# Query norms spread by one product with ones instead of a diagonal, a product and a copy; the order of the plan set anew

## The chip, the cores and the metric

One core of one Trainium2 chip. The metric is the device time of one execution in microseconds (us); the profile covers one such execution and gives its span, from the first to the last instruction. Engines: TensorE (PE; PEld is its weight load), VectorE (DVE), ScalarE (ACT), GpSimd (POOL) and SyncE (SP), which here issues most of the DMAs.

## The reference, cut to what matters

Channel attention followed by a feed-forward net. Per batch (4 of them, 6080 tokens, 256 channels) the columns of q and k are divided by their norms over the tokens, `s = kn^T qn / tau` (256x256) goes through a softmax over its rows, and the attention matrix is multiplied with v:

```
qn = q / (norm(q, axis=1) + 1e-6);  kn = k / (norm(k, axis=1) + 1e-6)
a  = softmax(kn.T @ qn / tau)            # 256 x 256 per batch
x  = (v @ a).reshape(24320, 256)
out = (relu(x @ w_in) ** 2) @ w_out      # w_in 256x2048, w_out 2048x256
```

The change touches the part that turns the raw scores `k^T q` into `s`: every score is multiplied by one over the norm of its key channel (its row, a number per partition) and by one over the norm of its query channel (its column, the same row of 256 numbers on every partition).

## The kernel before, in words

All 24320 tokens are worked in 24 chunks (six per batch) and 8 pairs of hidden blocks per chunk, so 192 pairs, "quads" in the code. The attention matrix is folded into w_in once per batch, so a quad is products of v with folded weights (L714), relu, square, and products with w_out (L861). Products of two 2x2 block matrices use seven products in place of eight, and each fp32 number is split in a high and a low fp32r half (`split`, L340: a cast on ACT or DVE, then a subtraction on DVE), three products per pair of operands.

A planner in the kernel (class `Plan`, L55 to L240) writes the order out by hand. Each step (`add`) has a key, which is a place on a time axis where 1.0 is one quad, a set of engines that may run it with a cost in us for each, and what it reads and writes. PE, SP and POOL take the ready step with the lowest key that lies no further than `PLACE["ahead"]` beyond the next PE step; DVE and ACT take the one that is due first, worked back from PE's order. The result is a fixed list; on the chip every engine runs its list in order and waits where an input is late. So a step that takes longer than its cost in the plan holds everything behind it on its engine. The table `PLACE` (L22) holds the keys and offsets.

For batch 0 the start of the kernel loads k and q (L345), multiplies them in plain fp32 (L469, each product recorded as two instructions), and adds their squares on DVE (L447); meanwhile PE also takes early score products of batch 1 (tile o). For batches 1 to 3 the scores are collected while the quads of the batch before run (b=1 during batch 0 and so on), and the steps `norms`, `spread`, `exps`, `attnT` and `fold` for the next batch lie between the quads.

`norms` (L496): DVE adds the two halves of the squares (L500), PE sums them over the partitions by four products with one column of ones (L505), which gives [128, 4], the squared norms of two key and two query halves, one channel per partition. ACT takes the root (L512) and, on a dummy, an exp to load the next table (L515). DVE does seven small operations on 4 columns (L520 to L526, two of them reciprocals: a Newton step for the root, then the inverse), then makes two diagonal matrices (L529) of the query factors. `spread` (L533): PE multiplies ones with the diagonals (L537), so that every partition holds all 256 query factors, and ACT or DVE copies them (L317) to the tile zq. `exps` (L543): DVE multiplies the scores by both factors (L550) and takes the row maximum (L552), ACT does the exp (L555). `attnT` (L565) transposes on PE (L572), `fold` (L596, L607) multiplies with w_in.

The PSUM tile h has two buffers, shared by the quads' products and by the tiles of these steps; a buffer is free for the next product only when its last reader is done. Names such as h or g in the profile are tiles; several steps of helpers share one line (L342 is the subtraction of every split, L317 every copy and cast).

Of the kernel before, what the change touches and what calls it, by code (L numbers as in the profile page):

```python
# [15 lines left out]
AF = mybir.ActivationFunctionType  # L16
# [3 lines left out]
P = 128  # L20

PLACE = {'ahead': {'P': 2.08, 'A': 1.179, 'V': 1.2, 'S': 2.311, 'G': 2.0},  # L22
 'shy': {'V': 0.964},
 'look': 5,
 'push': 6.141,
 'bias': {'V': 0.0, 'A': 0.956},
 'later': (0.86, 0.5),
 'scores': (2.0, 1.23, 0.632, 0.301, 0.646, 2.436),
 'folds': (3.331, 4.0, 0.599, 0.454, 1.234, 1.7),
 'tokens': (-3.119, -2.668, -2.352, -0.817, -0.655, -0.6, -0.55),  # L30
 'weights': (1.573, -0.172),
 'behind': (3, 3),
 'sums': (0.872, 1.889, 2.975, 3.873, 4.9, 5.812, 6.84),
 'lead': 13,
 'start': (-0.157, -0.107, 0.46, 0.864, 1.067, 1.201, -0.301, -0.25, -0.1, 0.02, 0.472),
 'groups': ((0, 1, 2), (3, 4, 5, 6)),
# [206 lines left out]
def vec(n):  # L243
    return 0.07 + 0.00104 * n
# [6 lines left out]
def act(n):  # L251
    return 0.1 + 0.00083 * n
# [3 lines left out]
def tile_channel_attention_relu2_ffn(ctx, tc, kq, vT, tau, w_in, w_out, outT):  # L256
# [236 lines left out]
    def tiny(key, eng, cost, fn, r, w):  # L493
        add(key, {eng: cost}, lambda e: fn(), r, w)

    def norms(key, b):  # L496
        acc, bank = ("acc", b), plan.tile("h", ("nb", b))
        ny, nz, nd = (plan.tile("y", (k, b, k)) for k in ("y1", "y2", "zv"))
        diag = plan.tile("zq", ("diag", b))
        alu(key, 512, lambda: nc.vector.tensor_add(out=made[acc][:, 0], in0=made[acc][:, 0], in1=made[acc][:, 1]),  # L500
            [(acc, 0)], [(acc, 0)])

        def sums():
            for i in range(2 * NH):
# [5 lines left out]
        def roots():  # L510
            y = get(ny, [P, 2 * NH])
            nc.scalar.activation(out=y, in_=made[bank][:, :2 * NH], func=AF.Sqrt)  # L512

        tiny(key, "A", 1.7 if b else 0.3, roots, [(bank, 0)], [(ny, 0)])
# [16 lines left out]
        tiny(key, "V", 1.9, scales, [(bank, 0), (ny, 0), ("rtau", 0)], [(nz, 0), (nd, 0), (diag, 0)])  # L531

    def spread(key, b):  # L533

        diag, bank = ("diag", b), plan.tile("h", ("zb", b))
        zq = plan.tile("zq", ("zqs", b))
        tiny(key, "P", 0.45, lambda: nc.tensor.matmul(  # L537
            out=get(bank, [P, HMAX])[:, :C], lhsT=ones, rhs=made[diag].rearrange("p d c -> p (d c)"),
            start=True, stop=True), [(diag, 0)], [(bank, 0)])
        add(key, {"A": act(256), "V": vec(256)}, lambda e: copy(e, get(zq, [P, NH, P]).rearrange("p d c -> p (d c)"),  # L540
                                                               made[bank][:, :C]), [(bank, 0)], [(zq, 0)])

    def exps(key, b, s, stok):  # L543
        zq, zv, den = ("zqs", b), ("zv", b, "zv"), plan.tile("den", ("den", b))
        for h in range(NH):
            en, nm = plan.tile("e", ("e", b, h)), plan.tile("nm", ("nm", b, h))

            def scaled(h=h, en=en, nm=nm):
                e = get(en, [P, C])
                nc.vector.scalar_tensor_tensor(out=e, in0=s()[:, h * C:(h + 1) * C], scalar=made[zv][:, h:h + 1],  # L550
                                               op0=ALU.mult, in1=made[zq].rearrange("p d c -> p (d c)"), op1=ALU.mult)
                nc.vector.tensor_reduce(out=get(nm, [P, 1]), in_=e, op=ALU.max, axis=AX.X, negate=True)  # L552

            tiny(key, "V", 0.95, scaled, [(zq, 0), (zv, 0), *stok], [(en, 0), (nm, 0)])
            tiny(key, "A", 0.6, lambda h=h, en=en, nm=nm: nc.scalar.activation(  # L555
# [115 lines left out]
    def v_split(keys, ci):  # L671
# [10 lines left out]
        b11, b12, b21, b22 = ((v, h, t) for h in range(2) for t in range(2))  # L682
        sub, plus = nc.vector.tensor_sub, nc.vector.tensor_add
        alu(keys[0], T, lambda: sub(out=one(), in0=blk(0, 1), in1=blk(0, 0)), [b11, b12], [(t1, 0)])
        for key, i, fn, hv, tok, x, y, r in zip(
# [123 lines left out]
    def weight_sums(key, i):  # L809
# [181 lines left out]
    for i, (b, g) in enumerate(loads):  # L991
        at(-6.9 + 0.25 * g if b == 0 else -0.9 + 0.05 * g, first_load, i, b, g)
    s0, s1 = plan.tile("x", ("s0",)), plan.tile("o11", ("s1",))
# [49 lines left out]
    for b in range(1, B):  # L1043
# [102 lines left out]
```

## Time and profile before

| | |
|---|---|
| times of three runs | 2065.6, 2067.95, 2067.96 us; median 2067.95 |
| the profiled execution | 2064.93 us, its span 2063.0 us |
| PE busy | 2048.0 us, 99% of the span |
| DVE busy | 1990.6 us, 96% |
| ACT busy | 1715.3 us, 83% |
| DMA | 562.51 MB, mean 273 GB/s |
| granted TensorE clock | 1.0 |

Busy time is the union of an engine's instructions. In a timeline a row merges neighbouring instructions of one line: start, duration of the row, and in brackets the idle time of the engine before it and what ended it. Matmuls overlap one another in such a row, so the pitch of PE's work is read from one row's start to the next.

### The profile page before, as it was taken

Reading aid. Unit: us, or ns where it says so; the run is one execution under the profiler, and the core shown is the slowest. Engines: PE = TensorE matmul, PEld = TensorE weight load, DVE = VectorE, ACT = ScalarE, POOL = GpSimd, SP = SyncE. Lnnn points to the kernel's source line nnn. Section 1 sums busy time; section 2 is a strip of 40 time slices with the busy share of each in tenths; the row PEclk is TensorE's granted clock in tenths of the full one; section 3 lists DMA queues with packets and bytes.
Section 4 is the critical chain, followed back from the end, with each engine's and each line's share of the span. In section 5 each row is a group of like instructions: output and inputs, shape, how many; then the busy total and the mean of one; then the engine's idle time right before and its main releaser. Section 6 shows DMA issues by size and latency. Waiting matters only on the chain.

```text
span 2063.0 us, 29286 instructions
## 1 busy us (share of the span) xinstructions
PE 2048.0 (99%) x9419; PEld 1714.0 (83%) x9419; DVE 1990.6 (96%) x3199; ACT 1715.3 (83%) x2718; POOL 188.2 (9%) x220
## 2 busy tenths in 40 slices
PE   9999999999999999999999999999999999999998
PEld 7778888888888888888888888888888888888887
DVE  7999999999999999999999999999999999999998
ACT  6779898988898889898888888989888787787785
POOL 0000001100111111100011111110000000000010
PEclk9999999999999999999999999999999999999999
DMA  9979989878999999978899999997898887887885
GB/s 362 346 231 351 292 258 304 231 230 278 296 320 309 286 300 282 283 232 252 275 297 319 302 288 293 290 285 229 254 274 271 278 244 224 244 247 224 241 230 156
DMA packets 342249, 562.51 MB, mean 273 GB/s; under 512 B 27088, under 2 KB 240336, under 8 KB 342096
## 3 DMA queue, kind: packets, MB, share of 16 engines
q1 hardware_dynamic: 311424, 491.09, 70.2%
q0 software_dynamic: 30672, 69.55, 19.2%
q8 instruction: 76, 1.25, 0.2%
q14 instruction: 77, 0.63, 0.1%
HBM read 424.02 MB, written 66.98 MB: 238 GB/s over the span
## 4 chain that ended last, share of the span: by engine, by line
PE 97%; DVE 1%; ACT 1%; issue 0%; DMA 0%; SPq 0%; DVEq 0%; ACTq 0%
PE h L714 25%; PE o L861 24%; PE h L861 20%; PE z L714 12%; PE x L714 6%; PE x L469 6%; PE h L607 2%; PE o L469 1%; DMA kq<-kq 0%; ACT s L321 0%; DVE uM L908 0%; DVE hl L342 0%; DVE uM L969 0%; DVE D L752 0%; PE h L505 0%
## 5 line engine op out<-in xcount | busy, mean ns | idle before, releaser
L714 PE MATMUL h<-vt,wt 128*128 128x512 f32 (+1 forms) x2304 | 617.5, 389 | 3.7 <-ACT x L317 2.7
L714 PEld LDWEIGHTS h<-vt,wt 128*128 128x128 f32 x2304 | 429.6, 188 | 92.0 <-ACT x L317 4.2
L861 PE MATMUL o<-g,wo 128*128 128x512 f32 (+1 forms) x1746 | 466.4, 388 | 0.1
L861 PE MATMUL h<-hl,wo 128*128 128x512 f32 (+1 forms) x1608 | 392.8, 388 | 0.0
L861 PEld LDWEIGHTS o<-g,wo 128*128 128x128 f32 x1746 | 327.2, 188 | 66.4 <-DVE g L342 1.3
L861 PEld LDWEIGHTS h<-hl,wo 128*128 128x128 f32 x1608 | 301.2, 188 | 60.6 <-ACT m L317 0.4
L342 DVE TENSOR_TENSOR hl<-D,hl 128x512 fp32r<-128x512 f32 (+1 forms) x536 | 350.0, 675 | 0.4
L714 PE MATMUL z<-vt,wt 128*128 128x512 f32 (+1 forms) x1152 | 324.4, 390 | 1.1 <-ACT z L317 0.8
L342 DVE TENSOR_TENSOR g<-s,g 128x1024 fp32r<-128x1024 f32 (+1 forms) x225 | 271.0, 1204 | 3.8 <-ACT g L317 3.8
L476 POOL DMA_DIRECT2D D<-D x159 | 140.7, 903 | 1414.6 <-DVE hl L342 795.9
L714 PEld LDWEIGHTS z<-vt,wt 128*128 128x128 f32 x1152 | 213.7, 188 | 46.6 <-DVE D L752 2.3
L321 ACT ACTIVATE D<-D 128x1024 f32<-128x1024 f32 (+1 forms) x159 | 167.4, 1053 | 89.8 <-DVE D L752 89.6
L317 ACT CAST hl<-D 128x512 fp32r<-128x512 f32 (+1 forms) x408 | 237.4, 618 | 5.4 <-PE h L861 4.2
L321 ACT ACTIVATE s<-s 128x1024 f32<-128x1024 f32 (+1 forms) x225 | 237.4, 1057 | 4.9 <-DVE s L752 4.2
L714 PE MATMUL x<-vt,wt 128*128 128x512 f32 (+1 forms) x576 | 161.2, 388 | 0.0
L327 ACT ACTIVATE s<-z 128x512 f32<-128x512 f32 (+1 forms) x192 | 113.3, 590 | 34.1 <-PE z L714 33.0
L317 ACT COPY x<-h 128x512 f32<-128x512 f32 (+1 forms) x192 | 110.5, 575 | 29.2 <-PE h L714 24.5
L861 PE MATMUL o<-t,wo 128*128 128x512 f32 (+1 forms) x477 | 133.6, 388 | 0.0
L317 ACT CAST g<-s 128x1024 fp32r<-128x1024 f32 (+1 forms) x126 | 131.1, 1042 | 0.4
L714 PEld LDWEIGHTS x<-vt,wt 128*128 128x128 f32 x576 | 108.1, 188 | 21.8
L327 ACT ACTIVATE s<-x 128x512 f32<-128x512 f32 (+1 forms) x192 | 114.3, 596 | 7.1 <-PE x L714 3.3
L317 ACT COPY m<-h 128x512 f32<-128x512 f32 (+1 forms) x192 | 111.5, 581 | 3.4 <-PE h L714 2.2
(136 smaller groups left out, 2965.6 us busy)
## 6 DMA issues: line engine op xcount, KB each, us to landing
wt<-wsc SPq DMA_DIRECT2D x368, 256.0 KB, 5.8
wt<-wsc SPq DMA_DIRECT2D x184, 384.0 KB, 5.2
wo<-wod_M SPq DMA_DIRECT2D x268, 256.0 KB, 4.2
wo<-wos SPq DMA_DIRECT2D x159, 384.0 KB, 4.9
kq<-kq SPq DMA_DIRECT2D x87, 512.0 KB, 6.9
D<-D POOLq DMA_DIRECT2D x131, 256.0 KB, 5.7
wsc<-wt SPq DMA_DIRECT2D x32, 896.0 KB, 6.2
acc<-sq POOLq DMA_DIRECT2D x54, 512.0 KB, 7.6
```

Source lines behind the costliest of these rows:

```text
L317: (nc.scalar.copy if e == "A" else nc.vector.tensor_copy)(out=out, in_=in_)
L321: nc.scalar.activation(out=out, in_=in_, func=AF.Square)
L327: nc.scalar.activation(out=out, in_=in_, func=AF.Relu)
L342: add(key, {"V": vec(n)}, lambda e: nc.vector.tensor_sub(out=l(), in0=x(), in1=h()), (*r, *wh), wl)
L469: nc.tensor.matmul(out=s[:, h * C:(h + 1) * C], lhsT=l, rhs=r, start=first and h == 0 and n == 0, stop=last and n == len(terms) - 1, skip_ ...
L476: add(key, {"G": 1.0}, lambda e: nc.gpsimd.dma_start(out=out(), in_=in_(), accum_op=ALU.add), r, w, size)
L607: nc.tensor.matmul(out=get(bank, [P, HMAX]), lhsT=made[aT][:, l, d, cs], rhs=made[w][:, r, d, :], start=n == 0, stop=n == 3 * NH - 1)
L714: nc.tensor.matmul(out=out[:, :T], lhsT=made[w][:, l, i], rhs=made[v][:, r, :T], start=start and n == 0, stop=n == 2, skip_group_check=True)
L861: nc.tensor.matmul(out=o[:, :T], lhsT=l, rhs=x[:, :T], start=start and k == 0, stop=stop and k == 2)
```

## The change

`norms` now makes the query part in its final, spread form: one product of the matrix of ones (as weights) with the 256 columns of squares of q puts the squared norm of every query channel on every partition; only the two key halves still use a product with one column of ones. The result is 258 columns wide, and the root, the Newton step and the reciprocals run on all 258. The diagonals, the step `spread` with its product and copy, and the tile zq go; the factors are kept in the unused half of the tile of squares. The planner's costs become 2.0 for the DVE step (1.9 before) and 0.5 or 1.9 for the root (0.3 or 1.7).

```diff
 def norms(key, b):
-        ny, nz, nd = (plan.tile("y", (k, b, k)) for k in ("y1", "y2", "zv"))
-        diag = plan.tile("zq", ("diag", b))
+        ny = plan.tile("y", ("y", b, "y"))
+        W = NH + C
...
-            for i in range(2 * NH):
-                nc.tensor.matmul(out=get(bank, [P, HMAX])[:, i:i + 1], lhsT=made[acc][:, 0, i * P:(i + 1) * P],
-                                 rhs=ones[:, 0:1], start=True, stop=True)
+            n2 = get(bank, [P, HMAX])
+            nc.tensor.matmul(out=n2[:, C:], lhsT=ones, rhs=made[acc][:, 0, C:], start=True, stop=True)
+            for i in range(NH):
+                nc.tensor.matmul(out=n2[:, C - NH + i:C - NH + i + 1], lhsT=made[acc][:, 0, i * P:(i + 1) * P],
+                                 rhs=ones[:, 0:1], start=True, stop=True, skip_group_check=True)
...
         def scales():
-            n2, y, z, x = made[bank][:, :2 * NH], get(nz, [P, 2 * NH]), get(nd, [P, 2 * NH]), made[ny]
-            nc.vector.tensor_scalar_max(out=y, in0=x, scalar1=1e-30)
+            y, z = made[ny], made[acc][:, 1, :W]
+            nc.vector.tensor_scalar_max(out=y, in0=y, scalar1=1e-30)
             nc.vector.reciprocal(out=z, in_=y)
-            nc.vector.tensor_mul(out=z, in0=z, in1=n2)
+            nc.vector.tensor_mul(out=z, in0=z, in1=n2())
             nc.vector.tensor_add(out=y, in0=y, in1=z)
             nc.vector.tensor_scalar(out=y, in0=y, scalar1=0.5, scalar2=1e-6, op0=ALU.mult, op1=ALU.add)
             nc.vector.reciprocal(out=z, in_=y)
             nc.vector.tensor_scalar_mul(out=z[:, :NH], in0=z[:, :NH], scalar1=rtau)
-            d = get(diag, [P, NH, P])
-            for i in range(NH):
-                nc.vector.tensor_scalar_mul(out=d[:, i], in0=ident, scalar1=z[:, NH + i:NH + i + 1])
...
-    def spread(key, b):
...
-    at(-0.69, spread, 0)
...
-        at(end + 1 + MID, spread, b)
```

The order is set anew through `PLACE`; two further switches, `raw` and `gv`, stand at values that leave their code unused. The entries that change:

```diff
-PLACE = {'ahead': {'P': 2.08, 'A': 1.179, 'V': 1.2, 'S': 2.311, 'G': 2.0},
+PLACE = {'ahead': {'P': 2.753, 'A': 1.179, 'V': 1.2, 'S': 2.402, 'G': 2.0},
- 'look': 5,
+ 'look': 4,
- 'bias': {'V': 0.0, 'A': 0.956},
+ 'bias': {'V': 0.048, 'A': 0.956},
- 'scores': (2.0, 1.23, 0.632, 0.301, 0.646, 2.436),
- 'folds': (3.331, 4.0, 0.599, 0.454, 1.234, 1.7),
- 'tokens': (-3.119, -2.668, -2.352, -0.817, -0.655, -0.6, -0.55),
+ 'scores': (1.82, 1.232, 0.72, 0.301, 0.646, 2.436),
+ 'folds': (3.331, 4.0, 0.599, 0.608, 1.234, 1.7),
+ 'tokens': (-3.167, -2.508, -2.352, -0.817, -0.655, -0.6, -0.55),
- 'start': (-0.157, -0.107, 0.46, 0.864, 1.067, 1.201, -0.301, -0.25, -0.1, 0.02, 0.472),
+ 'start': (-0.157, -0.107, 0.688, 0.748, 1.067, 1.201, -0.301, -0.25, -0.1, 0.02, 0.472),
-            (4, 5, 6): (7.248, 7.9, 7.6, 8.5)},
+            (4, 5, 6): (7.248, 7.9, 7.691, 8.736)},
+ 'open': (-0.86, -0.85, -0.62, -0.692, 0.106, -0.9, 0.05, 0.0, -0.66)}
...
-    at(-0.6, lambda key: decode_w_out(key, 0, 0.12))
+    at(PLACE["open"][3], lambda key: decode_w_out(key, 0, PLACE["open"][4]))
```

The other values of `open` are those that stood in the calls before.

## Rows read from the trace of the kernel before

**Rows 1.** The page: busy time, share of the span and number of instructions of each engine, and the chain of work that ended last, by engine.

```profile
PE 2048.0 (99%) x9419; PEld 1714.0 (83%) x9419; DVE 1990.6 (96%) x3199; ACT 1715.3 (83%) x2718; POOL 188.2 (9%) x220
...
PE 97%; DVE 1%; ACT 1%; issue 0%; DMA 0%; SPq 0%; DVEq 0%; ACTq 0%
```

**Rows 2.** Stretches of the run: from:to in us, its length, then busy us (instructions) of PE, PEld, DVE, ACT and POOL, the granted clock, the DMA share and GB/s. First stretches of 50 us, then three that begin just behind the DVE steps of batches 1 to 3.

```profile
0.00:50.00 50.00, 45.74 (x207) 39.76 (x207) 34.98 (x34) 30.61 (x31) 0.83 (x7) 1.00 0.96 360
50.00:100.00 50.00, 47.35 (x210) 38.60 (x211) 46.38 (x89) 37.46 (x63) 0.00 (x0) 1.00 0.94 344
100.00:150.00 50.00, 48.31 (x211) 39.16 (x211) 48.36 (x83) 37.50 (x59) 0.00 (x0) 1.00 0.70 234
...
397.00:410.00 13.00, 13.00 (x59) 10.53 (x58) 12.90 (x22) 13.00 (x24) 2.58 (x3) 1.00 0.86 240
904.00:930.00 26.00, 25.99 (x117) 21.19 (x117) 25.90 (x43) 23.52 (x42) 3.44 (x4) 1.00 0.80 225
1411.00:1437.00 26.00, 25.99 (x117) 21.23 (x116) 25.90 (x44) 23.89 (x42) 3.44 (x4) 1.00 0.80 223
```

**Rows 3.** All waits of PE in the run: who waited for whom, us in total, times, the longest. PE's first products of the run are the two that wait for a DMA; the four that wait for ACT lie between 92 and 122 us.

```profile
PE x L469 <- DMA kq<-kq: 4.3, 2, 3.6
PE h L714 <- ACT x L317: 2.7, 2, 1.7
PE z L714 <- ACT z L317: 0.8, 1, 0.8
PE h L714 <- ACT m L317: 0.8, 1, 0.8
PE h L714 <- DVE uM L908: 0.3, 1, 0.3
```

**Rows 4.** PE's timeline around the norms and the spread of batch 3.

```profile
1405.16 0.85 PE L714 MATMUL x<-vt,wt 128*128 128x512 f32 x3
1405.85 0.95 PE L505 MATMUL h<-ones,acc 128*128 128x1 f32 x8
1406.66 0.94 PE L714 MATMUL z<-vt,wt 128*128 128x512 f32 x3
1407.45 0.84 PE L714 MATMUL h<-vt,wt 128*128 128x512 f32 x3
...
1418.43 0.59 PE L537 MATMUL h<-zq,ones 128*128 128x256 f32 x2
1418.67 1.04 PE L714 MATMUL h<-vt,wt 128*128 128x512 f32 x3
1419.55 0.85 PE L861 MATMUL o<-g,wo 128*128 128x512 f32 x3
```

**Rows 5.** The instructions that read or write the tiles y and zq: line, engine, operation, tiles, count: shortest/median/longest ns, first and last start.

```profile
L529 DVE TENSOR_SCALAR zq<-ident,y x8: 277/280/282, 52.3 to 1410.7; 128x128 f32<-128x128 f32 x8
L550 DVE SCALAR_TENSOR_TENSOR e<-s_acc,y,zq x6: 474/476/477, 411.0 to 1426.6; 128x256 f32<-128x256 f32 x6
L520 DVE TENSOR_SCALAR y<-y x4: 156/158/170, 50.6 to 1409.1; 128x4 f32<-128x4 f32 x4
L522 DVE TENSOR_TENSOR y<-y,h x4: 157/158/159, 51.0 to 1409.5; 128x4 f32<-128x4 f32 x4
L523 DVE TENSOR_TENSOR y<-y x4: 161/161/164, 51.5 to 1409.7; 128x4 f32<-128x4 f32 x4
L524 DVE TENSOR_SCALAR y<-y x4: 169/170/171, 51.7 to 1409.9; 128x4 f32<-128x4 f32 x4
L526 DVE TENSOR_SCALAR y<-y,rtau x4: 228/229/230, 52.1 to 1410.3; 128x2 f32<-128x2 f32 x4
...
L317 ACT COPY zq<-h x3: 375/375/375, 404.3 to 1419.1; 128x256 f32<-128x256 f32 x3
```

**Rows 6.** The same view for reciprocals 1, 2 and 4 columns wide (L525, the second of the DVE step, has the row of L521 again, with a longest of 178).

```profile
L1005 DVE RECIPROCAL rtau<-tau_sb x1: 157/157/157, 16.7 to 16.7; 128x1 f32<-128x1 f32 x1
...
L561 DVE RECIPROCAL den<-den x4: 165/166/167, 58.4 to 1439.5; 128x2 f32<-128x2 f32 x4
...
L521 DVE RECIPROCAL y<-y x4: 177/178/179, 50.8 to 1409.3; 128x4 f32<-128x4 f32 x4
```

**Rows 7.** The same view for other DVE operations of 256 and 512 columns.

```profile
L552 DVE TENSOR_REDUCE nm<-e x8: 419/420/421, 55.8 to 1427.1; 128x1 f32<-128x256 f32 x8
...
L389 DVE TENSOR_SCALAR hl<-kq x12: 415/420/422, 66.7 to 146.9; 128x512 f32<-128x512 f32 x12
```

**Rows 8.** Timeline of batches 1 and 2, DVE and PE rows: one pair of batch 1, then a pair of batch 2, both behind the DVE step.

```profile
408.65 0.68 DVE L908 TENSOR_TENSOR uM<-h,uM 128x512 f32<-128x512 f32 x1
...
409.65 2.88 PE L861 MATMUL h<-hl,wo 128*128 128x512 f32 x12
...
910.05 1.22 DVE L342 TENSOR_TENSOR g<-s,g 128x1024 fp32r<-128x1024 f32 x1
...
912.19 0.85 PE L861 MATMUL o<-g,wo 128*128 128x512 f32 x3
```

**Rows 9.** Timeline of the start, from the norms of batch 0 to the low half of its attention matrix.

```profile
50.36 0.17 ACT L512 ACTIVATE y<-h 128x4 f32<-128x4 f32 x1 [2.19 <-PE h L505]
...
50.56 0.17 DVE L520 TENSOR_SCALAR y<-y 128x4 f32<-128x4 f32 x1
...
54.15 4.48 PE L469 MATMUL o<-kq 128*128 128x256 f32 x20
54.35 0.42 DVE L317 COPY zq<-h 128x256 f32<-128x256 f32 x1 [0.35 <-PE h L537]
...
55.29 0.48 DVE L550 SCALAR_TENSOR_TENSOR e<-x,y,zq 128x256 f32<-128x256 f32 x1
...
60.79 0.68 DVE L342 TENSOR_TENSOR aT<-h,aT 128x512 fp32r<-128x512 f32 x1
```

**Rows 10.** The start again: SP's first load of w_out, and PE's first product of batch 1's scores.

```profile
35.93 0.59 SPq L345 DMA_DIRECT2D vt<-w_out  x1
...
47.65 1.89 PE L469 MATMUL o<-D 128*128 128x256 f32 x8
```

More of the change, by code (lines that the diff above doesn't have):

```diff
@@ L47 @@
  'pieces': ((2, 5), (5, 7), (0, 2)),
- 'halved': 1}
+ 'halved': 1,
+ 'raw': 0,
+ 'gv': 99,
+ 'open': (-0.86, -0.85, -0.62, -0.692, 0.106, -0.9, 0.05, 0.0, -0.66)}
 class Op:
@@ L279, in tile_channel_attention_relu2_ffn @@
     RINGS = {"kq": 4, "g2": 2, "D": PLACE["rings"][1], "hl": 3, "t4": 1, "s": 3, "sq": 2, "wo": 4, "wt": 3, "vt": PLACE["rings"][0], "v": 1, "tt": 1,
-             "m7": 1, "uM1": 1, "uM5": 1, "uM6": 1, "uM7": 1, "acc": 1, "s_acc": 1, "zq": 1, "e": 2, "den": 2,
-             "aT": 1, "y": 3, "nm": 2,
+             "m7": 1, "uM1": 1, "uM5": 1, "uM6": 1, "uM7": 1, "acc": 1, "s_acc": 1, "e": 2, "den": 2,
+             "aT": 1, "y": 1, "nm": 2,
              "h": 2, "x": 1, "z": 1, "o00": 1, "o01": 1, "o10": 1, "o11": 1}
@@ L415, in decode_w_out @@
         Wn = decode(key, "out", g, "sq", lead)
+        if PLACE["raw"]:
+            store(key, lambda: dtile(("wraw", g), [P, 4, GW]), lambda: made[Wn], [(Wn, 0)], [(("wraw", g), 0)], 512)
         for i in range(2):
@@ L497, in norms, with n2 @@
         acc, bank = ("acc", b), plan.tile("h", ("nb", b))
-        ny, nz, nd = (plan.tile("y", (k, b, k)) for k in ("y1", "y2", "zv"))
-        diag = plan.tile("zq", ("diag", b))
+        ny = plan.tile("y", ("y", b, "y"))
         alu(key, 512, lambda: nc.vector.tensor_add(out=made[acc][:, 0], in0=made[acc][:, 0], in1=made[acc][:, 1]),
             [(acc, 0)], [(acc, 0)])
+        W = NH + C
         def sums():
-            for i in range(2 * NH):
-                nc.tensor.matmul(out=get(bank, [P, HMAX])[:, i:i + 1], lhsT=made[acc][:, 0, i * P:(i + 1) * P],
-                                 rhs=ones[:, 0:1], start=True, stop=True)
+            n2 = get(bank, [P, HMAX])
[3 more added lines that the diff above has]
+                                 rhs=ones[:, 0:1], start=True, stop=True, skip_group_check=True)
         tiny(key, "P", 0.9, sums, [(acc, 0)], [(bank, 0)])
[L510 to L514, printed above, removed]
+        def n2():
+            return made[bank][:, C - NH:]
+        tiny(key, "A", 1.9 if b else 0.5, lambda: nc.scalar.activation(out=get(ny, [P, W]), in_=n2(), func=AF.Sqrt),
+             [(bank, 0)], [(ny, 0)])
         tiny(key, "A", 1.5, lambda: nc.scalar.activation(out=root, in_=made[ny][:, 0:1], func=AF.Exp, scale=0.0),
@@ L526, in scales @@
             nc.vector.tensor_scalar_mul(out=z[:, :NH], in0=z[:, :NH], scalar1=rtau)
-            d = get(diag, [P, NH, P])
-            for i in range(NH):
-                nc.vector.tensor_scalar_mul(out=d[:, i], in0=ident, scalar1=z[:, NH + i:NH + i + 1])
-        tiny(key, "V", 1.9, scales, [(bank, 0), (ny, 0), ("rtau", 0)], [(nz, 0), (nd, 0), (diag, 0)])
-    def spread(key, b):
[L535 to L541, printed above, removed]
+        tiny(key, "V", 2.0, scales, [(bank, 0), (ny, 0), ("rtau", 0)], [(acc, "z"), (ny, 0)])
     def exps(key, b, s, stok):
-        zq, zv, den = ("zqs", b), ("zv", b, "zv"), plan.tile("den", ("den", b))
+        acc, den = ("acc", b), plan.tile("den", ("den", b))
         for h in range(NH):
@@ L549, in scaled @@
                 e = get(en, [P, C])
-                nc.vector.scalar_tensor_tensor(out=e, in0=s()[:, h * C:(h + 1) * C], scalar=made[zv][:, h:h + 1],
-                                               op0=ALU.mult, in1=made[zq].rearrange("p d c -> p (d c)"), op1=ALU.mult)
+                nc.vector.scalar_tensor_tensor(out=e, in0=s()[:, h * C:(h + 1) * C], scalar=made[acc][:, 1, h:h + 1],
+                                               op0=ALU.mult, in1=made[acc][:, 1, NH:NH + C], op1=ALU.mult)
                 nc.vector.tensor_reduce(out=get(nm, [P, 1]), in_=e, op=ALU.max, axis=AX.X, negate=True)
-            tiny(key, "V", 0.95, scaled, [(zq, 0), (zv, 0), *stok], [(en, 0), (nm, 0)])
+            tiny(key, "V", 0.95, scaled, [(acc, "z"), *stok], [(en, 0), (nm, 0)])
             tiny(key, "A", 0.6, lambda h=h, en=en, nm=nm: nc.scalar.activation(
@@ L683, in v_split @@
         sub, plus = nc.vector.tensor_sub, nc.vector.tensor_add
+        ahead = ci >= PLACE["gv"]
         alu(keys[0], T, lambda: sub(out=one(), in0=blk(0, 1), in1=blk(0, 0)), [b11, b12], [(t1, 0)])
@@ L690, in v_split @@
             src = one if hv is None else lambda hv=hv: blk(*hv)
-            if fn:
+            if ahead and i == S2:
+                pass
+            elif fn:
                 alu(key, T, lambda fn=fn, src=src, x=x, y=y: fn(out=src(), in0=blk(*x), in1=blk(*y)), [r, tok], [tok])
+            if ahead and i == S3:
+                gather(key + 0.001, lambda: blk(0, 0), lambda: blk(0, 1), [b11, b12], [b11], T // 2)
             t = plan.tile("vt", ("vt", ci, i))
@@ L819, in x @@
             return f()[:, 1, k]
-        alu(key, 512, lambda: nc.vector.tensor_add(out=f()[:, 0], in0=made[w][:, 0], in1=made[w][:, 1]),
-            [(w, 0), (w, 1)], [(fn_, "a")])
+        if PLACE["raw"]:
+            load(key - PLACE["raw"], lambda: f()[:, 0].rearrange("p (f e) c -> p f (e c)", f=2),
+                 lambda: dram["wraw", j // 2][:, j % 2::2, :], [(("wraw", j // 2), 0)], [(fn_, "a")], 256)
+        else:
+            alu(key, 512, lambda: nc.vector.tensor_add(out=f()[:, 0], in0=made[w][:, 0], in1=made[w][:, 1]),
+                [(w, 0), (w, 1)], [(fn_, "a")])
         for k, fn, a, b in ((0, nc.vector.tensor_add, (0, 3), (0, 1)), (1, nc.vector.tensor_sub, (0, 2), (1, 0)),
@@ L991, in tile_channel_attention_relu2_ffn @@
     for i, (b, g) in enumerate(loads):
[L992 removed]
+        at(-6.9 + 0.25 * g if b == 0 else PLACE["open"][5] + PLACE["open"][6] * g, first_load, i, b, g)
     s0, s1 = plan.tile("x", ("s0",)), plan.tile("o11", ("s1",))
@@ L1008, in tile_channel_attention_relu2_ffn @@
     at(-0.7, norms, 0)
-    at(-0.69, spread, 0)
     at(-0.68, lambda key: exps(key, 0, lambda: made[s0], [(s0, 0)]))
     at(-0.67, attnT, 0)
-    at(-0.86, lambda key: decode_w_in(key, 0, 0.0))
-    at(-0.66, fold_split, 0, 0)
+    at(PLACE["open"][0], lambda key: decode_w_in(key, 0, 0.0))
+    at(PLACE["open"][8], fold_split, 0, 0)
     at(-0.65, fold, 0, 0, 0, "z")
@@ L1016, in tile_channel_attention_relu2_ffn @@
     at(-0.63, lambda key: combine(key, 0, 0, 0.0))
-    at(-0.85, load_v, 0)
-    at(-0.62, lambda key: v_split([key] * 7, 0))
-    at(-0.6, lambda key: decode_w_out(key, 0, 0.12))
+    at(PLACE["open"][1], load_v, 0)
+    at(PLACE["open"][2], lambda key: v_split([key] * 7, 0))
+    at(PLACE["open"][3], lambda key: decode_w_out(key, 0, PLACE["open"][4]))
     for g in range(EARLY):
@@ L1027, in tile_channel_attention_relu2_ffn @@
     at(PLACE["start"][9] + PLACE["start"][10] + 0.02, lambda key: score_out(key, 1, s1))
-    at(PLACE["start"][6], lambda key: decode_w_in(key, 1, 0.0))
+    at(PLACE["start"][6], lambda key: decode_w_in(key, 1, PLACE["open"][7]))
     at(PLACE["start"][7], load_v, 1)
```

## The prediction

> **What bounds the kernel now.** I read the page first, then the stretches, then the timelines at the places that the change touches. The page shows PE busy 99% of the span and 97% of the chain of waits on PE; but DVE is busy 96% as well [rows 1]. The stretches say where PE is not full: 4.3, 2.7 and 1.7 us are missing in the first three stretches of 50 us, and PE's named waits are 4.3 us for the first loads, 4.3 for ACT's copies at 92 to 122 us and 0.3 for DVE [rows 3]; right behind the DVE steps of batches 1 to 3 PE is full, and DVE too, with 12.90 of 13, 25.90 of 26 and 25.90 of 26 us [rows 2]. So there are two prices in this kernel: PE work taken out of the full part is worth its own length, and DVE work put into it is worth its length less the distance by which DVE runs ahead of PE, because DVE has no idle time in which to catch up. The planner fixes the order; nothing moves out of the way of a step that takes longer than planned.
>
> **PE, four times.** Before batch 3's norms a row of three products has a pitch of 0.69 us. The eight instructions of L505 take 0.81 us to the next row, and that row takes 0.79 where its form takes 0.68, so 0.92 in all. The two of L537 take 0.24, and the row behind them 0.88, 0.20 too long: 0.44 [rows 4]. After the change the product with ones has the shape of L537, so 0.44, and four one-column instructions are left of eight, half of 0.92, so 0.46: 0.90 in place of 1.36. That frees 0.46 us a batch, 1.84 in all (bounds 0 and 4 x 0.92), and PE's time is the bound, so it counts.
>
> **DVE's step, four times.** Before: 158 + 178 + 158 + 161 + 170 + 178 + 229 ns and two diagonals of 279, so 1.79 us [rows 5, 6]. After: a maximum over 258 columns; 512 columns take 420 ns [rows 7], and with 157 ns for one column that gives 0.29. The product, with one operand in PSUM, 0.45, between the 420 and 476 ns of 256-column rows [rows 5, 7]; the sum 0.42; the operation with two scalars 0.30; the two-column product 0.23. There remain two reciprocals over 258 columns, and no row has one that wide. The narrow ones tell most: 157 ns at one column, 166 at two, 178 at four, each within 2 ns of itself in all its executions, while the other operations lie between 156 and 171 ns at four columns [rows 5, 6]. That is 7 ns for each further column, where the ordinary operations of rows 7 need one or a half. At 7 ns a reciprocal over 258 columns takes 0.157 + 257 x 0.007 = 1.96 us. Bounds: 0.42, the 256-column row of an ordinary operation [rows 7], and 2.48, from the 9 ns between one and two columns. I take 1.96, because it rests on the same operation. The step is then 0.29 + 1.96 + 0.45 + 0.42 + 0.30 + 1.96 + 0.23 = 5.61 us: 3.82 longer (bounds 0.74 and 4.86). The plan counts on 2.0 for it.
>
> [...]
>
> **What the longer step does to PE in batches 1 to 3.** Behind the step DVE's queue holds the quads' splits, sums and bank releases, and PE waits for those. How far is DVE ahead? In batch 1 the bank h is read by DVE until 409.33 and its next product starts at 409.65, 0.32 us later; in batch 2 g is ready at 911.27 and its product starts at 912.19, 0.92 later [rows 8]; batch 3 has batch 2's order, and I use 0.92 again. All three come within 15 us of the step, with DVE full between [rows 2, 8]. So PE stops for 3.82 - 0.32 = 3.5 and twice 3.82 - 0.92 = 2.9: 9.3 us. The step also keeps its PSUM bank until its third operation, which now ends some 2.2 us later (1.78 of the first reciprocal, 0.13 of the maximum, 0.29 of the product); a product that waits for the bank waits for a part of the same 3.82, so it isn't counted again.
>
> **The start.** The step begins at 50.56, the scaled scores (L550) at 55.29, after the diagonals, the product and the copy [rows 9]. Now the root over 258 columns takes 0.2 more (375 ns for a 256-column copy from PSUM on ACT against 173, [rows 5, 9]), then 5.61: L550 starts about 56.4, 1.1 us later. DVE has 3.82 more to do and 0.42 less for the copy, 3.4, before the last half of aT (60.79) that the first fold needs. PE has score products of batch 1 to do meanwhile (row at 54.15). Cost: nothing, if those cover it, up to 3.4; I take 2.2, the middle of 1.1 and 3.4.
>
> **The order.** The w_out load of the start comes ahead of one 512 KB load of k and q in SP's queue; w_out's was issued 12 us before PE's first product of batch 1 [rows 10], which hides the exchange; without that cover it would cost about the issue's 0.6 us. Its decoding moves forward with it. The folds of batch 0 move by +0.23 and -0.12 quads, those of later batches, the score norms, the first token splits and two bursts by 0.24 or less, and PE may look 0.67 of a quad further. What this can win is PE's idle time at 92 to 122 us, 2.7 + 0.8 + 0.8 = 4.3 [rows 3]; what it can lose I bound by as much again. I take a win of 1.2: these waits end with ACT's copies, which a longer look on PE doesn't make earlier. On ACT the root grows by 0.2 and three copies of 0.375 go; ACT isn't the bound.
>
> **The sum.** 9.3 + 2.2 - 1.84 - 1.2 = +8.5 us on the profiled execution's 2064.93: 2073.4. The three runs lie 2.2 above it on the mean (2067.2), so the time would be 2075.6, +0.4% on the median of 2067.95. With the bounds of the reciprocal, the start and the order this case runs from 2070 to 2081.
>
> **Rivals.** *A wide reciprocal costs what other operations do (0.42 us).* Then the step is 0.74 longer, batch 1 loses 0.4, batches 2 and 3 nothing, and in the start L550 comes 1.9 us earlier, of which I count 0.5, since PE had products to do; with PE's 1.84 and the order's 1.2 that is -3.1, so 2064.0: faster or the same. For it: four columns are few to draw a line from, and the plan's 2.0 is what such operations would add up to. Against it: the three widths of rows 6 lie on one slope. It decides as soon as a wide reciprocal takes under about 0.8 us, where the sum is zero. [...]
>
> *The step is long, but the new order gives it room*: it lies where DVE is ahead of PE or idle. Then the three batches cost nothing, and 2.2 - 1.84 - 1.2 = -0.8 gives 2066.3. For it: DVE has 72 us idle over the run [rows 1]. Against it: it has 0.1 us in each stretch behind the step [rows 2], the plan doesn't know of the 3.6 us, and the step is one piece.
>
> **Chances.** Forecast 0.62, the first rival 0.20, the second 0.18. About 0.2%, 4.1 us, is what can be told from no change here: faster is under 2063.8, slower over 2072.1. The forecast gives 0.58 slower and 0.04 the same; the first rival, centred on 2064.0, 0.12 faster and 0.08 the same; the second 0.04 faster, 0.12 the same and 0.02 slower. Together 0.16, 0.24, 0.60. The range of 2063 to 2081 takes in both rivals' centres and leaves out the rest of the first one's fast side and little above. The forecast's own range is 2070 to 2081.
>
> **What would show it.** Two rows of a 258-column reciprocal in each batch: near 2 us for the forecast, near 0.4 for the first rival. Rows of DVE's other wide operations of 0.29 to 0.45. Behind the step, PE rows with idle time released by DVE, together about 3 us within 20 us in each of batches 1 to 3, and PE busy lower in those stretches; no such idle time is the second rival. PE's L505 slot with six instructions of 0.9 us instead of 1.36 with L537. The sum is wrong if PE's idle time at 92 to 122 us changes by more than 4 us, or if new idle time stands where the moved steps are and not behind the norms.

## The result and the profile after

Over five runs each the changed kernel takes 2078.94 us on the median (2077.07 to 2082.05), the kernel before 2067.44 (2065.6 to 2067.96): a ratio of 1.0061, with a 95% interval from 1.0049 to 1.0072. That is 11.5 us more, where 8.5 were forecast. The profiled execution took 2079.77 us, its span 2077.7; that is 14.8 over the profiled execution of before, since it also lost some 3 us at its first loads (its 33rd product starts at 15.89 us, in that one at 13.11).

The page of the kernel after, the lines that answer to [rows 1]:

```profile
PE 2054.3 (99%) x9403; PEld 1717.3 (83%) x9403; DVE 2008.1 (97%) x3196; ACT 1714.1 (82%) x2709; POOL 189.7 (9%) x220
...
PE 88%; DVE 6%; DMA 3%; ACT 2%; issue 1%; SPq 0%; DVEq 0%; ACTq 0%
```

PE has 16 instructions fewer and yet is busy 6.3 us longer, and the chain of waits now runs through DVE for 6% of the span where it had 1%. DVE's busy time grew by 17.5 us; four steps that are 3.41 us longer make 13.6 of these.

The root on ACT and the seven operations of the DVE step, after, from the views of the tiles y and acc (shortest/median/longest ns; they answer to [rows 5, 6]):

```profile
L520 ACT ACTIVATE y<-h x4: 387/387/389, 53.1 to 1417.1; 128x258 f32<-128x258 f32 x4
L527 DVE TENSOR_SCALAR y<-y x4: 289/290/298, 56.0 to 1420.4; 128x258 f32<-128x258 f32 x4
L528 DVE RECIPROCAL acc<-y x4: 1766/1766/1767, 56.3 to 1420.7; 128x258 f32<-128x258 f32 x4
L529 DVE TENSOR_TENSOR acc<-acc,h x4: 423/424/425, 58.2 to 1422.5; 128x258 f32<-128x258 f32 x4
L530 DVE TENSOR_TENSOR y<-y,acc x4: 428/428/429, 58.7 to 1422.9; 128x258 f32<-128x258 f32 x4
L531 DVE TENSOR_SCALAR y<-y x4: 295/296/297, 59.1 to 1423.4; 128x258 f32<-128x258 f32 x4
L532 DVE RECIPROCAL acc<-y x4: 1766/1766/1768, 59.4 to 1423.7; 128x258 f32<-128x258 f32 x4
L533 DVE TENSOR_SCALAR acc<-acc,rtau x4: 228/228/230, 61.2 to 1425.5; 128x2 f32<-128x2 f32 x4
```

The two reciprocals take 3.53 of the step's 5.20 us (0.290 + 1.766 + 0.424 + 0.428 + 0.296 + 1.766 + 0.228). Between 4 and 258 columns a reciprocal gains (1766 - 178) / 254 = 6.25 ns per column.

All waits of PE after, against [rows 3]:

```profile
PE x L474 <- DMA kq<-kq: 4.4, 2, 3.5
PE z L713 <- DVE s L751: 2.9, 1, 2.9
PE o L864 <- DVE g L345: 2.6, 4, 1.1
PE h L864 <- DVE uM L911: 2.6, 2, 1.3
PE h L566 <- ACT e L549: 2.2, 2, 1.9
PE h L713 <- ACT x L320: 1.2, 2, 0.6
PE z L713 <- ACT z L320: 1.0, 3, 0.5
```

Before, DVE kept PE waiting for 0.3 us in all; now it does for 8.1 (2.9 + 2.6 + 2.6), and the transposes of batch 0 (L566) wait 2.2 for the exp. The named waits for ACT's copies fell from 4.3 to 2.2 [rows 3].

PE's timeline after, behind the DVE step of batch 1 and of batch 2 (start, duration of the row; in brackets the idle time before it), against [rows 8]:

```profile
404.63 2.88 PE L864 MATMUL h<-hl,wo 128*128 128x512 f32 x12
410.37 0.97 PE L713 MATMUL z<-vt,wt 128*128 128x512 f32 x3 [2.86 <-DVE s L751]
...
913.79 2.88 PE L864 MATMUL h<-hl,wo 128*128 128x512 f32 x12
...
919.61 0.50 PE L864 MATMUL o<-g,wo 128*128 128x512 f32 x1 [1.13 <-DVE g L345]
921.42 4.43 PE L864 MATMUL h<-hl,wo 128*128 128x512 f32 x12 [1.30 <-DVE uM L911]
```

Batch 1 shows one stop of 2.86 us, batch 2 two that add up to 2.43. And there is something else: the same twelve products take 2.88 us at 913.79 and 4.43 at 921.42. Why, the stretches of the kernel after say (PE, PEld, DVE, ACT, POOL busy, granted clock, DMA share, GB/s):

```profile
404.00:410.00 6.00, 3.51 (x16) 2.58 (x14) 5.90 (x12) 4.73 (x10) 0.00 (x0) 1.00 0.56 177
410.00:416.00 6.00, 5.63 (x25) 4.66 (x26) 6.00 (x12) 4.45 (x8) 1.72 (x2) 1.00 0.58 129
...
918.00:921.00 3.00, 0.98 (x4) 0.25 (x2) 2.99 (x5) 3.00 (x8) 1.27 (x2) 1.00 0.84 216
921.00:924.50 3.50, 3.08 (x7) 2.51 (x8) 3.36 (x6) 0.31 (x2) 0.52 (x2) 0.51 0.97 177
...
1432.50:1436.00 3.50, 3.06 (x7) 2.40 (x8) 3.39 (x6) 0.40 (x2) 0.52 (x2) 0.58 0.97 175
...
65.00:68.00 3.00, 3.00 (x9) 2.44 (x9) 2.99 (x5) 1.72 (x3) 0.00 (x0) 0.55 0.87 321
```

PE had 0.98 us of work from 918 to 921; from 921 to 924.5 the granted clock is 0.51 on the mean. Before, the stretch behind this step had a clock of 1.00 [rows 2]. The fall adds 4.43 - 2.88 = 1.55 us to the stop. Batch 3 is like batch 2 (0.58 from 1432.5 to 1436, and 4.62 us for the same twelve products at 1432.94), while batch 1, with the longest single stop, stays at 1.00. In the start the clock is 0.55 from 65 to 68 us, and the timeline of the start, which answers to [rows 9], has a stop ahead of it:

```profile
53.12 0.39 ACT L520 ACTIVATE y<-h 128x258 f32<-128x258 f32 x1 [1.83 <-PE h L512]
...
55.76 0.20 ACT L522 ACTIVATE root<-y 128x1 f32<-128x1 f32 x1
...
56.00 0.30 DVE L527 TENSOR_SCALAR y<-y 128x258 f32<-128x258 f32 x1 [0.22 <-ACT root L522]
...
61.99 0.48 DVE L544 SCALAR_TENSOR_TENSOR e<-x,acc 128x256 f32<-128x256 f32 x1
...
63.70 0.41 PE L566 MATMUL h<-ident,e 128*128 128x128 f32 x2 [1.88 <-ACT e L549]
...
64.94 3.27 PE L474 MATMUL o<-kq 128*128 128x256 f32 x8
```

Eight score products take 3.27 us behind the stop; eight of the same form took 1.89 before [rows 10]. The difference is 1.38 us, at a granted clock of 0.55.

### The profile page after: what moved, and what is told of

Its sections match the earlier page's. It is cut to its first block, busy times and chain, and to the rows that moved or that the text cites. A ratio compares the mean times of both kernels' runs of the same rounds, so it can differ in the third digit from the quotient of the medians.

```text
span 2077.7 us, 29225 instructions
## 1 busy us (share of the span) xinstructions
PE 2054.3 (99%) x9403; PEld 1717.3 (83%) x9403; DVE 2008.1 (97%) x3196; ACT 1714.1 (82%) x2709; POOL 189.7 (9%) x220
## 4 chain that ended last, share of the span: by engine, by line
PE 88%; DVE 6%; DMA 3%; ACT 2%; issue 1%; SPq 0%; DVEq 0%; ACTq 0%
PE h L713 23%; PE o L864 22%; PE h L864 20%; PE z L713 12%; PE x L713 6%; PE x L474 4%; PE h L601 2%; DMA kq<-kq 2%; DVE hl L345 1%; DVE g L345 1%; DVE D L751 1%; PE o L474 1%; DVE acc L452 0%; DMA vt<-w_in 0%; DVE acc L532 0%
## 5 line engine op out<-in xcount | busy, mean ns | idle before, releaser
L320 ACT CAST hl<-D 128x512 fp32r<-128x512 f32 (+1 forms) x420 | 245.2, 617 | 14.5 <-PE h L864 10.5
L320 ACT COPY z<-h 128x512 f32<-128x512 f32 (+1 forms) x192 | 112.1, 584 | 4.1 <-PE h L713 3.1
```

The source lines that it names most:

```text
L320: (nc.scalar.copy if e == "A" else nc.vector.tensor_copy)(out=out, in_=in_)
```

## The experiments

Times are medians of four to twelve runs, each beside runs of the kernel before on the same chip (2066.54, 2067.74 and 2066.89 us in the three groups e1 to e4, e5 to e8, e9 to e11). Differences to the kernel before are taken within a group; where runs of two groups are compared, it is by this difference, and the 95% interval is then some 3 us to either side. e1, e8 and e10 leave out a part of the norms' arithmetic, e5 and e9 the Newton step, the 1e-6 and the guard against zero; they tell about time alone. The theory: the DVE step is longer, because two reciprocals over 258 columns are slow, and what lies behind it on DVE holds PE up. The first rival: the form is harmless and the order or the plan's wrong cost makes the loss.

**e1, the reciprocals made short.** Order and everything else stay.

```diff
-            nc.vector.reciprocal(out=z, in_=y)
+            nc.vector.tensor_scalar_max(out=z, in0=y, scalar1=1e-30)
...
-            nc.vector.reciprocal(out=z, in_=y)
+            nc.vector.tensor_scalar_max(out=z, in0=y, scalar1=1e-30)
```

> The two 258-column reciprocals of the DVE step are replaced by a maximum with a constant of the same width, 0.29 us each; the inverse of the norms is left out, so the scores are scaled by other numbers. Plan and order are those of the changed kernel. Theory (the length of the step is the price): the step falls from 5.2 to 2.25 us, PE's waits behind it in batches 1 to 3 (3.6, 4.8 and 4.9 us above the usual pitch) and in the start go almost wholly: 2064 to 2068 us. Rival (the new order costs the time): 2074 to 2080.

Measured: 2065.35 us, ratio 0.9993 (0.9985 to 1.0002). The step is 2.3 us, and the loss is gone: 12.7 us between e1 and the changed kernel, each taken against its own runs of the kernel before. PE's waits in e1 name DVE for 0.5 us in all:

```profile
PE x L474 <- DMA kq<-kq: 4.5, 2, 3.5
...
PE o L864 <- DVE g L345: 0.5, 2, 0.3
```

**e11, the long step put into the kernel before.** The other direction: form, order and diagonals of before, and two dummies ahead of the step's first operation (in the kernel the three calls stand on one line).

```diff
+            nc.vector.reciprocal(out=made[acc][:, 1, :258], in_=ones[:, 0:1].to_broadcast([P, 258]))
+            nc.vector.reciprocal(out=made[acc][:, 1, :258], in_=ones[:, 0:1].to_broadcast([P, 258]))
             nc.vector.tensor_scalar_max(out=y, in0=x, scalar1=1e-30)
```

> The kernel before, with its order and its diagonals, and two reciprocals over 258 columns (of ones, into the unused half of the squares) ahead of the DVE step's first operation, each about 1.77 us: the step is 5.3 us in place of 1.79, 3.5 longer, close to the 3.82 of the prediction, and nothing else is changed. By the prediction's terms 3 x (3.5 - 0.3 to 0.9) + 2 = 10.4 us: 2076 to 2080, up to 2084 with the halved clock behind the stops. If the new form's other parts (product with ones, order) make the loss: 2067 to 2070.

Measured: 2079.47 us, ratio 1.0059 (1.0046 to 1.0072), so 12.6 us for a step 3.52 longer (the dummies take 1760 ns each). The length of the step makes the loss in the old order as well. It is at the upper end of what the terms gave. PE's waits that end with the step or with DVE's work behind it, in batches 1 to 3, are 4.4 + 2.1 + 1.2 = 7.7 us, where growth less lead gives 3.2 + 2.6 + 2.6 = 8.4; another 1.9 lie in the start. PE's largest wait for DVE, then its timeline, which shows the stops of batches 1 and 2 as the prediction describes them, several short ones that are released by DVE:

```profile
PE h L714 <- DVE y L522: 4.4, 3, 1.5
...
404.96 1.62 PE L714 MATMUL h<-vt,wt 128*128 128x512 f32 x6 [1.46 <-DVE y L522]
...
412.49 0.70 PE L537 MATMUL h<-zq,ones 128*128 128x256 f32 x2 [1.14 <-DVE uM L908]
...
422.53 1.65 PE L714 MATMUL h<-vt,wt 128*128 128x512 f32 x6 [0.39 <-DVE uM L908]
...
916.01 0.94 PE L714 MATMUL h<-vt,wt 128*128 128x512 f32 x3 [1.47 <-DVE y L522]
...
923.60 0.70 PE L537 MATMUL h<-zq,ones 128*128 128x256 f32 x2 [0.50 <-DVE uM L908]
```

The first of them waits for the product of L522, by which the step gives its PSUM bank back; 4.4 of the 7.7 us are such waits. The granted clock is 1.00 in the start and behind the stops, so a loss of this size needs no fall of the clock.

**e10, one reciprocal left.** Only the second is replaced, as in e1.

> The changed kernel with its order kept; the second wide reciprocal is replaced by a 258-column maximum (0.29 us), so the inverse is left out and the DVE step is 3.7 us in place of 5.2. Steps of 2.3, 5.2 and 7.0 us gave 2065.4, 2078.9 and 2088.8 us. If the loss follows the step's length beyond a small lead: 2070 to 2074. If a step of 3.7 us still hides behind DVE's lead and the loss sets in only with the halved clock: 2065 to 2068.

Measured: 2069.99 us, ratio 1.0015 (1.0006 to 1.0024): 3.1 us over before, at the lower edge of what the theory gave. The profiled execution is the slowest of its eleven (2073.8 us). PE's longest waits for DVE are 1.4 and 1.2 us, and the clock stays at 1.00 behind them and in the start. Stretches of e10 behind its stop in the start and around those of batch 2:

```profile
64.00:68.00 4.00, 3.79 (x17) 2.85 (x17) 4.00 (x7) 2.02 (x4) 0.00 (x0) 1.00 1.05 385
...
913.00:918.00 5.00, 3.75 (x17) 2.80 (x16) 4.97 (x9) 4.22 (x10) 1.72 (x2) 1.00 0.93 181
918.00:924.00 6.00, 5.53 (x25) 4.26 (x24) 6.00 (x11) 5.15 (x9) 0.86 (x1) 1.00 0.84 178
```

**e4, a third reciprocal.** The second is written twice.

> The changed kernel with its second reciprocal done twice with the same input and output: the step grows by 1.77 to 7.0 us, the plan is the same. Theory (length of the step, PE loses what goes beyond a fixed lead of DVE): each of batches 1 to 3 loses 1.3 to 1.8 more, the start 1 to 1.8: 2083 to 2087 us. Rival (order): within 2 us of the changed kernel's 2078.9.

Measured: 2088.81 us, ratio 1.0108 (1.0095 to 1.0121), so 22.3 us over before and more than expected. PE's waits grow with the step (4.6 us at once in batch 1), and now batch 1 has its own fall of the clock too. Stretches of e4 behind the step of batch 1:

```profile
404.00:410.00 6.00, 2.22 (x10) 1.50 (x8) 5.90 (x11) 3.01 (x8) 0.00 (x0) 1.00 0.42 143
410.00:416.00 6.00, 5.13 (x15) 4.10 (x16) 5.02 (x9) 2.97 (x6) 1.72 (x2) 0.72 0.50 104
```

In one order, steps of 2.3, 3.7, 5.2 and 7.0 us are thus -1.2, +3.1, +11.5 and +22.3 us against before. The first 1.5 us cost 4.3, the next 1.5 cost 8.4 and the last 1.8 cost 10.8. If PE stopped for all that is added, four steps longer by 1.5 us would cost 6 us. From 3.7 to 5.2 us the cost is 2.4 us more than that, and from 5.2 to 7.0 it is 10.8 where all that is added makes 7.1. The kernel with 3.7 us has no fall of the clock (1.00 in e10's stretches), the one with 5.2 has three of 1.38 to 1.74 us, and the one with 7.0 has one in batch 1 too (0.72, beside 0.58 from 922 to 928 and 0.86 from 1434 to 1440). That fits, but the difference of 2.4 us lies within what the medians can tell; the falls themselves are shown by the rows.

**e8, short only in the start.** As e1, but for batch 0 alone.

```diff
-            nc.vector.reciprocal(out=z, in_=y)
+            if b:
+                nc.vector.reciprocal(out=z, in_=y)
+            else:
+                nc.vector.tensor_scalar_max(out=z, in0=y, scalar1=1e-30)
```

> The changed kernel with the two reciprocals replaced by a maximum of the same width in batch 0 alone (batch 0's scores are scaled by other numbers); batches 1 to 3 keep them. Tells the start's share from that of the later batches: theory from the traces, the start's share is 3 to 5 us, so 2073 to 2076; if the start has none 2078 to 2080; if it has all 2066 to 2069.

Measured: 2074.65 us, ratio 1.0034 (1.0021 to 1.0047), 6.9 over before. So the two reciprocals of the start cost 11.5 - 6.9 = 4.6 us and the six of batches 1 to 3 cost 6.9 + 1.2 = 8.1, each give or take some 3 us.

**e3, the new order with the old form.** Only `PLACE` and the call of `decode_w_out` that reads it are the changed kernel's.

```diff
-PLACE = {'ahead': {'P': 2.08, 'A': 1.179, 'V': 1.2, 'S': 2.311, 'G': 2.0},
+PLACE = {'ahead': {'P': 2.753, 'A': 1.179, 'V': 1.2, 'S': 2.402, 'G': 2.0},
...
```

> The norms, spread and diagonals of the kernel before with the order values of the changed kernel. Theory (length of the step): no long step, so 2062 to 2070 us, which is what the order alone is worth. Rival (order): 2074 to 2080.

Measured: 2062.77 us, ratio 0.9981 (0.9973 to 0.9990): the order is worth 3.8 us, and this version beats both kernels. PE's waits:

```profile
PE h L717 <- ACT x L320: 1.0, 3, 0.6
PE z L717 <- ACT z L320: 1.0, 3, 0.5
PE o L864 <- DVE g L345: 0.6, 2, 0.5
```

Against [rows 3], the 4.3 us for ACT's copies have become 2.0 (the wait for the first loads, 3.9, is left out here).

**e2, the new form with the old order.** The opposite edit, the old values of `PLACE` in the changed kernel.

> The norms of the changed kernel with every order value of the kernel before. Theory (length of the step): the step is still 5.2 us and planned at 2.0, so 2074 to 2081 us, with PE idle behind the step. Rival (order): 2064 to 2069.

Measured: 2089.91 us, ratio 1.0110 (1.0097 to 1.0123), outside of both expectations. The stops behind the norms are there, but some 9 us are lost where neither expectation had them, at 613 to 656 us, between batches 1 and 2. ACT's and PE's timeline and a stretch of e2:

```profile
633.07 1.06 ACT L324 ACTIVATE sq<-kq 128x1024 f32<-128x1024 f32 x1 [3.42 <-DMA kq<-kq]
...
634.67 2.93 PE L474 MATMUL x<-hl 128*128 128x256 f32 x12 [3.73 <-ACT x L320]
```

```profile
630.00:640.00 10.00, 6.27 (x24) 5.19 (x23) 5.01 (x8) 3.77 (x6) 0.86 (x1) 0.68 0.99 281
```

DVE is idle half of the time there, so it isn't the long step that binds. The planner made another list from the new form's steps and costs. In this one ACT stands 3.42 us for a load of k and q (kq) ahead of the copy of x for which PE then waits 3.73, and the clock falls behind that (0.68 as the mean of the stretch). Why the load is late wasn't separated. The two changes don't add up: the order alone is worth -3.8 us, the form in the old order +23.4, both together +11.5.

**e6, the plan told the true cost.**

```diff
-        tiny(key, "V", 2.0, scales, [(bank, 0), (ny, 0), ("rtau", 0)], [(acc, "z"), (ny, 0)])
+        tiny(key, "V", 5.1, scales, [(bank, 0), (ny, 0), ("rtau", 0)], [(acc, "z"), (ny, 0)])
```

> The changed kernel with 5.1 in place of 2.0 as the planner's cost of the DVE step. Theory (the plan is wrong by 3 us and queues PE's needs behind the step): the plan brings work ahead of the step or gives splits to ACT, part of the waits goes: 2067 to 2075 us. If DVE has no room whatever the plan knows: 2076 to 2081.

Measured: 2074.74 us, ratio 1.0033 (1.0021 to 1.0046), 7.0 over before. A plan that knows the cost wins 4.5 us, but not the rest. Over the whole run it gave ACT no more to do (1709.2 us busy against 1714.1). Its PE stops behind the norms of batches 1 to 3 are shorter, 1.6 at most, and the mean granted clock of its five runs is 0.999 to 1.0, as in the kernel before (0.998 to 1.0), where the changed kernel has 0.996 and 0.997. So the falls of the clock, 1.38 to 1.74 us each in the changed kernel, may be most of what it won.

**e7, the true cost, and the step of batches 1 to 3 cut in seven.** Each of the step's operations becomes a step of the plan with its own cost, so that splits can go between them.

> As the run with the true cost, and in batches 1 to 3 the step is cut into its seven operations, each a step of the plan with its own cost, so that DVE may do other work between them. Theory (one piece of 5 us is the trouble, more than DVE's 3.4 us of added work): waits behind the norms nearly go, 2063 to 2071 us. If the added work itself is the price: 2073 to 2080.

Measured: 2078.11 us, ratio 1.0049 (1.0036 to 1.0062): missed. Behind the norms of batches 1 to 3 PE's named waits are short, 0.68 at most, yet counted above the usual pitch of its products it still loses 2.5 to 2.7 us a batch. By the same count the new list loses 3.5 us around 600 and 8.0 around 1100 us, where a score product waits 2.7 for ACT (the kernel before loses 1.0 at each). It doesn't show whether cutting the step could help, since the list changed as a whole.

**e5 and e9, no reciprocal at all.** ACT makes the inverse norm as exp(-0.5 ln n2). In e5 the planner made a new list; e9 keeps the list of the changed kernel and has both functions in the place of the root:

```diff
-        tiny(key, "A", 1.9 if b else 0.5, lambda: nc.scalar.activation(out=get(ny, [P, W]), in_=n2(), func=AF.Sqrt),
-             [(bank, 0)], [(ny, 0)])
...
+        def roots():
+            y = get(ny, [P, W])
+            nc.scalar.activation(out=y, in_=n2(), func=AF.Ln)
+            nc.scalar.activation(out=made[acc][:, 1, :W], in_=y, func=AF.Exp, scale=-0.5)
...
+            z = made[acc][:, 1, :NH]
+            nc.vector.tensor_scalar_mul(out=z, in0=z, scalar1=rtau)
```

> The inverse root of the 258 columns is made on ACT as exp(-0.5 ln(n2)), two operations in place of the root, and DVE keeps only the two-column product; the Newton step, the 1e-6 and the guard against a norm of zero are left out. The product with ones stays, the order values are those of the changed kernel. Theory (DVE's long step is the price): DVE's step is 0.23 us, so no wait behind it, PE has its 0.46 us a batch and the order its 3.8: 2057 to 2064 us. Rival (the spread by ones or the order costs): 2072 or more.

Measured: 2069.69 us, ratio 1.0020 (1.0009 to 1.0031): missed. There is no stop over 1 us behind the norms, but the new list loses 6.8 us at 600 to 650, here too with a fall of the clock, behind a wait of 1.6 us for ACT. Two stretches of e5:

```profile
600.00:608.00 8.00, 5.13 (x20) 3.14 (x18) 8.00 (x14) 5.11 (x9) 2.13 (x3) 1.00 1.05 301
608.00:612.00 4.00, 3.65 (x9) 2.78 (x9) 1.50 (x3) 2.01 (x5) 1.35 (x2) 0.57 1.11 256
```

> The changed kernel with its order of instructions kept, but with the inverse norms made by ACT: Ln over 258 columns, then Exp with scale -0.5 in the place of the root and of the dummy exp, so that DVE's step is the two-column product alone (0.23 us in place of 5.2). It leaves out the Newton step, the 1e-6 and the guard against zero. If the long DVE step is the whole loss: no PE stop above 1 us behind the norms of batches 1 to 3, the start about 4 us shorter than in the changed kernel, and 2058 to 2065 us. If the order of the changed kernel is itself worse with this form of the norms: 2068 or more, as in the earlier kernel with Ln and Exp whose order had been planned again (2069.7).

Measured: 2063.53 us, ratio 0.9982 (0.9973 to 0.9991). With the list kept, the DVE step of 0.22 us and two functions on ACT beat both kernels by 3.4 and 15 us. So e5's loss was its list, and the form without a wide reciprocal costs no time in the kept one. It isn't better than e3 (2062.77) by more than these runs can tell.

## Why the prediction was right

**The step.** Every operation but the reciprocals came within 0.03 us of its forecast. The reciprocals measured 1.77 in place of 1.96: the line through 1, 2 and 4 columns [rows 6] was right in kind, its 7 ns per column too steep by 0.75. The step grew by 3.41, not 3.82.

**PE's stops in batches 1 to 3.** The rule was growth less DVE's lead. With the measured growth it gives 3.41 - 0.32 = 3.1 and twice 3.41 - 0.92 = 2.5; the timelines show 2.86, and 2.43 in batch 2. e11, in the order in which the leads were read, gives 7.7 for the three batches where the rule gives 8.4. So the leads read from [rows 8] were near the right ones, and the term of 9.3 would have been 8.1 with the right reciprocal. What the prediction lacked is the price of a stop beyond its idle time: the clock of 0.51 and 0.58 behind it in batches 2 and 3, 1.55 us in batch 2 and 1.74 in batch 3. The times give 8.1 us for these three batches (e8 against e1), the two traces 9.3; the traces count 10.7 at the norms less 1.4 that e1 loses, and the changed kernel doesn't, around 600 us. That offset, and with it the exact 8.1, looks like chance of where short waits fall; this isn't shown.

**The start.** This term was too small: 2.2 forecast, 4.6 measured. PE's idle time ahead of the transposes is 2.2 us (1.88 and 0.35). That it is just what was forecast is luck, for the forecast was the middle between two bounds. The rest goes to the clock of 0.55 behind the stop, a fall that the prediction didn't count here either: product by product, PE of the changed kernel is 0.2 us behind e1's ahead of the transposes and 4.5 behind it after the eight slow score products. So the traces leave little of the 4.6 open.

The date was wrong as well: the scaled scores begin at 61.99 and not at 56.4. Half of that is no matter of the step: the root starts at 53.12 in place of 50.36 [rows 9], since this execution is 2.8 us late from its first loads on. Then the step begins 2.5 us after the root's end at 53.5, where before it began 0.03 after. Its first operation now writes the root's tile y in place, which the dummy exp (L522, behind a table load of 1.28 us) still reads; before, L520 wrote another tile. The bracket at 56.00 names this wait with 0.22 us only; the rest of the 2.5 is other DVE work that the list puts ahead. A version without this dependence wasn't tried, and e1 and e8 have it as well, so it isn't in the 4.6.

**PE's saving.** Its size was right. The timeline of PE at batch 1's norms, after:

```profile
394.17 0.59 PE L510 MATMUL h<-acc,ones 128*128 128x256 f32 x2
394.60 0.50 PE L512 MATMUL h<-ones,acc 128*128 128x1 f32 x4
394.96 0.94 PE L864 MATMUL o<-g,wo 128*128 128x512 f32 x3
395.75 0.85 PE L713 MATMUL z<-vt,wt 128*128 128x512 f32 x3
```

From 394.17 to 395.75 are 1.58 us, of which 0.68 is the usual pitch of a row [rows 4]: 0.90, as forecast. But it didn't come out as time. With the order of the changed kernel the old form takes 2062.77 (e3) and the new form with short operations 2065.35 (e1): 2.6 more and not 1.84 less. In the traces, PE of e1 loses 1.9 us more in the first 100 us (half of it at the first loads, ahead of any norms), 1.2 around 600, and 1 each behind the norms of batches 2 and 3. DVE of e1 is busy 7.2 us longer than that of e3 (1996.1 and 1988.9), of which four steps 0.47 longer make 1.9, and ACT 4.5 less (1713.2 and 1717.7): the list of the new form gives DVE some work that ACT had. That e9, with next to no DVE step, isn't faster than e3 either, says that DVE's length isn't all of it. Whether this shift of work eats the saving wasn't tested; the lists of the two forms differ all over, and the 2.6 itself is little above what the medians can tell.

**The order.** Win forecast 1.2, measured 3.8 (e3); 2.3 us of it are the waits for ACT's copies, the place that the prediction named, though it counted on little more than a fourth of what there was to win.

**The sum.** In the prediction's parts, forecast against measured: order -1.2 and -3.8; form without the long reciprocals -1.84 and +2.6; batches 1 to 3 +9.3 and +8.1; start +2.2 and +4.6. Together +8.5 and +11.5. The step from the profiled execution to the median was 2.2 and is 2.5 with the five runs. The sign and the main term stood on the right mechanism; the single terms were off by up to 4.4 us, and two errors of 2.6 and 4.4 with opposite signs made the sum look better than its parts. That the sum came so near is in part luck.

**The rivals.** That a wide reciprocal costs what other operations do fell with L528 (1766 ns, where the step's other operations on 258 columns take 290 to 428); e1 shows what it would have meant: -1.2 us, where the rival gave -3.1. That the new order gives the step room fell with the stops of 2.9 and 2.4 us and with e11: the same length costs 12.6 us in the old order.

## What to carry to other kernels

An operation that costs about what its neighbours do on 4 columns (the reciprocal: 178 ns, they 158 to 170) may cost four to six times as much on 258 (1766 against 290 to 428): draw the line through the widths that the trace has before trusting that it is as cheap as its neighbours, and keep a reciprocal narrow, ahead of the spread and not behind it, or give its work to another engine. On DVE, here 97% busy and all but full behind the step, 3.41 us of added time became stops of PE of 2.86 and 2.43 us, about the added time less the lead with which DVE ran ahead (0.32 and 0.92), and that lead can be read from two rows. In a kernel whose list is planned, compare variants in a kept list; a changed cost makes a new list, and that moved the time by more (e2, e5, e7) than most edits.

## What was not expected of the hardware

The granted clock of TensorE fell to about half behind short stops: 0.51 behind 1.13 and 1.30 us of idle time with one product between (batch 2), 0.58 in batch 3 behind 1.15 and 1.30, 0.55 in the start behind 1.88 and 0.35. It didn't fall behind one stop of 2.86 us (batch 1, 1.00 from 404 to 416), nor behind stops of 1.46 and 1.14 with some 6 us of work between them (e11, 1.00 from 404 to 416), nor behind e11's stop of 1.9 us in the start (1.00 from 56 to 72), but it did in batch 1 when the stop was 4.6 (e4, 0.72 as the mean of 6 us). e2 and e5 have falls behind stops far from the norms (0.68 as the mean from 630 to 640, 0.57 from 608 to 612). In e10 it was 1.00 behind its stops of 1.2 and 1.4 us. What tells these cases apart wasn't tested. The three falls of the changed kernel cost 1.38, 1.55 and 1.74 us (start, batches 2 and 3), each more than half of the idle time ahead of it (2.23, 2.43 and 2.45).
